# A second expert's weight load moved into the loop, the widest layer 1 block put first, registers read ahead, and fills placed anew

## The chip, the core and the metric

The kernel runs on one core of a Trainium2 chip. The metric is the device time of one execution in microseconds (us). Three timed runs of the kernel before gave 604.38, 605.06 and 607.2 us; the median is 605.06 us. A profiled execution, taken apart from these, took 608.49 us, and its span from the first to the last instruction is 606.7 us.

## The reference

Two stages are computed in float32. The first is a linear attention for 8 batches, 8 heads, 576 positions and a head size of 64; the second sends each of the 4608 resulting rows (512 wide) to the one expert of 8 that its gate prefers, and multiplies the expert's result by the gate's weight.

```python
q_s = softmax(q, axis=-1);  k_s = softmax(k, axis=2)
kv  = einsum('bhsd,bhse->bhde', k_s, v)
x   = einsum('bhsd,bhde->bhse', q_s, kv)      # 4608 rows of 512
expert_idx = argmax(x @ w_gate, axis=1);  gate_w = softmax(x @ w_gate)[expert_idx]
for e in range(8):                            # rows sorted by expert
    h = maximum(x_sorted[lo:hi] @ w1[e], 0)   # layer 1: 512 -> 1024
    y_sorted[lo:hi] = h @ w2[e]               # layer 2: 1024 -> 512
out = gate_w[:, None] * y                     # in the order of the rows
```

## The kernel before, in words

**First part (0 to 190 us of the span).** A planner (class `Plan`) knows every step of the attention, the routing and the first expert's start by a name, a batch and an index (`KM2.1.0` is step KM2 of batch 1). From costs and due times it writes one fixed order for each engine. Before a step on TensorE it can put fills: products of a matrix of ones, 384 columns wide, whose results nobody reads (line 227). The table `FILL` lists how many stand ahead of which step: `KM2.1.0.18` means 18. The finished rows are scattered to a table `xs` in device memory, sorted by expert. For the first expert the first 384 rows are loaded early, and layer 1 for them and a third of layer 2 belong to this part (lines 755 and 769).

**Second part (from 190 us on), function `experts`.** Each engine has its own program here, and semaphores tie them together. Before the loop TensorE does the other two thirds of the first expert's layer 2 (`first`, line 1131), and between them the 12 transposes of the loop's first tile of rows (line 1147). Then each engine walks a loop, one round for a tile of up to 384 rows. A table `tab` in SBUF, computed by the routing, holds for each round its width in units of 32 rows (`kind`, 1 to 12), its first row, and whether a new expert begins; engines read it into registers (line 1009).

In a round TensorE branches on `kind` to one of six blocks of code for layer 1: `tiny1` for up to 64 rows, or `layer1(w)` for a width of 256, 288, 320, 352 or 384. Every `layer1(w)` has 96 products (8 blocks of hidden units, 12 products each). After it come the three thirds of layer 2: 24 products (`layer2`) or 16 (`half`) for each 128 rows that the tile has. ScalarE applies the relu to each hidden block (line 1194), VectorE computes its low part (line 1281, semaphore `sHL[f]`). In the middle of the round VectorE transposes the next tile (line 1260), ScalarE rounds it (line 1178), and VectorE takes the low part (line 1266, semaphore `sXL`, on which the next round's layer 1 waits). ScalarE scales the results (line 1163), and GpSimd scatters them to the output (line 1368).

Weights are 2 MB for each layer of an expert, and come by SyncE's queue into `RAW1` and `RAW2` (lines 1420 and 1424), from which ScalarE and VectorE make the high and low parts W1H, W1L (lines 1231, 1334), W2H and W2L (lines 1187, 1272). The loop's first rounds belong to the first expert, whose weights have been there since the first part. SyncE loads the loop's first tile, then, before its loop, both weights of the second expert:

```python
with e.If(x.get(LIVE, 1, 0, 1) > 0):          # line 1445
    wload(x.get(EO, 1, 0, E - 1), False)
```

In each round it waits until the tile in use has been taken over (`sGS`), loads the next tile's rows (line 968), and, in the first round of a new expert, loads the weights of the one after, each when its buffer is free.

ScalarE begins a round with three reads of the table into registers (`kind`, `fresh`, `turn`) and does a fourth after the relus.

Of the kernel before, what the change touches and what calls it, by code (L numbers as in the profile page):

```python
# [16 lines left out]
P = 128  # L17
# [25 lines left out]
            T4=135.561, T5=67.264, T6=-338.231, T7=192.024, T8=-120.773, T9=1000.0, PD=179.626, SW=73.996)  # L43
WINDOW = 0.0
FILL = """
KM2.0.0.17 KM4.0.0.1 KM2.1.0.18 KM4.1.0.4 KV.0.0.1 KV.0.1.1 KM2.2.0.13 G2.0.0.1 KV.1.1.1 KV.1.2.1 KM2.3.0.4 G0.1.0.7
KM4.3.0.1 TR.1.2.1 KV.2.2.1 R5.0.0.2 MM.1.4.4 KV.3.2.1 G0.3.0.9 TR.3.2.1 G2.3.0.2 KV.4.0.1 KV.4.1.1 KV.4.2.1 KM2.5.0.16
KV.4.3.2 R5.2.0.1 MM.3.0.1 MM.3.1.2 MM.3.2.2 MM.3.3.2 TR.3.4.2 G2.4.0.2 KV.5.2.1 G2.5.0.2 MM.5.0.4 MM.5.1.4 TR.5.4.1
KM4.7.0.14 KV.6.0.1 KV.6.1.1 KV.6.2.1 G0.6.0.5 TR.6.2.2 IT.4.1.1 IT.4.2.4 MM.7.0.1 MM.7.4.2 KV.7.0.1 KV.7.1.1 KV.7.2.2
"""  # L50
KD, ROW, LW, EO, LIVE = range(5)
PE, DVE, ACTE, POOL, SP = "pe", "dve", "act", "pool", "sp"
# [919 lines left out]
def experts(nc, tc, g):  # L972


    NC, NF, DM, N, E = g.NC, g.NF, g.DM, g.N, g.E
# [3 lines left out]
    H2, Q = P // 2, P // 4  # L979
# [9 lines left out]
    sPH, sHH, sHL = [sem(x, NF) for x in ("sph", "shh", "shl")]  # L989
# [29 lines left out]
    def pe():  # L1019
        x = Eng(nc.tensor, "pe")  # L1020
        e = nc.tensor
# [37 lines left out]
        def tiny1():  # L1059
            for h in range(2):  # L1060
                e.wait_ge(sW1[2 * h], it)
                e.wait_ge(sW1[2 * h + 1], it)
                n = 0
                for c in range(NC):
                    for wt in (W1H, W1L):
                        m = e.matmul(g.PH[h], g.XH[:, c, :P], wt[:, c, h * DM:(h + 1) * DM], start=(n == 0), stop=(n == 2 * NC - 1))
                        if n == 0 and h == 0:
                            m.wait_op(sXL, it, GE)
                        n += 1
                m.then_inc(sPH[h], 1)  # L1070
            ones(4)
            for h in range(2):
                if h:
                    ones(3)
                for f in range(4 * h, 4 * h + 4):
                    m = e.matmul(TP[h][:, f - 4 * h, :], HS[:, f * P:(f + 1) * P], g.pair, start=True, stop=True)
                    if f == 4 * h:
                        m.wait_op(sHH[h], it, GE)
                m.then_inc(sPH[2 + h], 1)
            for f in range(4, NF):  # L1080
                e.sem_inc(sPH[f], 1)
# [18 lines left out]

        def body(j):
            kind = x.get(KD, j, 0, 12)
            with e.If(kind < 9):
                with e.If(kind < 3):
                    tiny1()
                with e.If(kind > 2):
                    layer1(2 * P)
            with e.If(kind > 8):
                with e.If(kind < 12):
                    with e.If(kind < 11):  # L1110
                        with e.If(kind < 10):
                            layer1(9 * Q)
                        with e.If(kind > 9):
                            layer1(10 * Q)
                    with e.If(kind > 10):
                        layer1(11 * Q)
                with e.If(kind > 11):
                    layer1(3 * P)
            for u in range(3):
                with e.If(kind > 4 * u + 2):  # L1120
                    layer2(u)
                with e.If(kind < 4 * u + 3):
                    with e.If(kind > 4 * u):
                        half(u)
            x.add("it", 1)
# [15 lines left out]
        it, hc = x.reg("it", 1), x.reg("hc", 1)  # L1141
# [10 lines left out]
    def act():  # L1152
        x = Eng(nc.scalar, "act")
        e = nc.scalar
        it, m1, m2 = x.reg("it", 1), x.reg("m1", 16), x.reg("m2", 16)
        cu = [x.reg(f"c{u}", 1) for u in range(3)]
        ou = [x.reg(f"o{u}", 16) for u in range(3)]

        def yout(u, again=True):
            if again:  # L1160
                e.wait_ge(sO[u], ou[u])
                x.add(f"o{u}", 16)
            m = e.activation(g.YT[u], g.PY[u], AF.Copy, scale=g.GA[:, u:u + 1]).wait_op(sPY[u], cu[u], GE)  # L1163
            m.then_inc(sYT[u], 1)
            x.add(f"c{u}", 1)

        def yhalf(u):
            e.wait_ge(sO[u], ou[u])
            x.add(f"o{u}", 16)
            for i, cols in enumerate(HALVES):  # L1170
                m = e.activation(g.YT[u][:H2, cols], g.PY[u][H2:, cols], AF.Copy, scale=g.GA[:H2, u:u + 1])
                if i == 0:
                    m.wait_op(sPY[u], cu[u], GE)
                m.then_inc(sYH, 1)
            x.add(f"c{u}", 1)

        def evac(to=g.XH, src=g.XR):
            e.activation(to, src, AF.Copy).wait_op(sT, it, GE).then_inc(sXH, 1)

        def gates():  # L1180
            e.wait_ge(sGS, it)
            for u in range(3):
                e.wait_ge(sYT[u], cu[u])
            e.activation(g.GA, g.GS[:, :, 0], AF.Copy).then_inc(sGA, 1)

        def w2_hi(f):
            m = e.activation(W2H[:, f, :], g.RAW2[:, f, :], AF.Copy)  # L1187
            if f == 0:
                m.wait_op(sR2, m2, GE)
            m.then_inc(sH2[f], 1)  # L1190

        def relus(split):
            for f in range(NF):
                e.activation(g.HH[:, f, :], g.PH[f][:, :W], AF.Relu).wait_op(sPH[f], it, GE).then_inc(sHH[f], 1)  # L1194
                if f == 0:
                    gates()
                if split:
                    w2_hi(f)

        def tiny(split):  # L1200
            w2 = (lambda *fs: [w2_hi(f) for f in fs]) if split else (lambda *fs: None)
            w2(0)
            e.activation(HS[:, :DM], g.PH[0], AF.Copy).wait_op(sPH[0], it, GE).then_inc(sHH[0], 1)
            w2(1)
            gates()
            w2(2)
            for h in range(2):
                e.activation(g.HH[:, 4 * h:4 * h + 4, :H2], TP[h], AF.Relu).wait_op(sPH[2 + h], it, GE).then_inc(sHH[2 + h], 1)
                w2(3 + h)
            w2(5, 6, 7)  # L1210
            for f in range(4, NF):
                e.sem_inc(sHH[f], 1)

        def body(j):
            kind = x.get(KD, j, 0, 12)
            fresh = x.get(LW, j, 0, 1)
            turn = x.get(LW, j + 1, 0, 1)
            for run in (tiny, relus):
                with e.If(kind > 2 if run is relus else kind < 3):
                    with e.If(fresh > 0):  # L1220
                        run(True)
                        x.add("m2", 16)
                    with e.If(fresh < 1):
                        run(False)
            x.add("it", 1)
            with e.If(x.get(KD, j + 1, 0, 12) > 0):
                evac()
            with e.If(turn > 0):
                for q in range(NQ):
                    sl = slice(2 * q * P, 2 * (q + 1) * P)  # L1230
                    m = e.activation(W1H[:, :, sl], g.RAW1[:, :, sl], AF.Copy)
                    if q == 0:
                        m.wait_op(sR1, m1, GE)
                    m.then_inc(sH1[q], 1)
                x.add("m1", 16)
            for u in range(3):
                with e.If(kind > 4 * u + 2):
                    yout(u)
                with e.If(kind < 4 * u + 3):
                    with e.If(kind > 4 * u):  # L1240
                        yhalf(u)

        for u in range(3):
            e.sem_inc(sYT[u], 1)
        yout(0, again=False)
        yout(1, again=False)
        evac(g.XH.rearrange("p c (u t) -> p u c t", t=P), g.PT)
        yout(2, again=False)
        x.walk(body)
        for u in range(3):  # L1250
            e.sem_inc(sSp2, 1).wait_op(sO[u], ou[u], GE)
# [141 lines left out]
    def sp():  # L1393
        x = Eng(nc.sync, "sp")
        e = nc.sync
# [33 lines left out]
        def body(j):  # L1429
            e.wait_ge(sGS, it)  # L1430
            rows(j + 1)
            with e.If(x.get(LW, j, 0, 1) > 0):
                x.add("k", 1)
                kk = e.snap(k, min_val=2, max_val=E)
                with e.If(x.get(LIVE, kk, 0, 1) > 0):
                    wload(x.get(EO, kk, 0, E - 1), True)
            x.add("it", 1)

        n, row = g.AT0
        for u in range(3):  # L1440
            with e.If(n > 4 * u):
                e.dma_start(g.XT[:, u, :], g.xs[bass.ds(row + u * P, P), :]).then_inc(sX, 16)
            with e.If(n < 4 * u + 1):
                e.sem_inc(sX, 16)
        with e.If(x.get(LIVE, 1, 0, 1) > 0):
            wload(x.get(EO, 1, 0, E - 1), False)
        x.walk(body)

    pe()
# [35 lines left out]
```

## Time and profile before

| what | value |
|---|---|
| timed runs | 604.38, 605.06, 607.2 us; median 605.06 us |
| profiled execution | 608.49 us; span 606.7 us |
| TensorE products busy | 575.0 us, 95% of the span |
| VectorE, ScalarE, GpSimd busy | 323.3, 237.0, 130.9 us |
| mean granted TensorE clock | 0.986 of full speed |
| data moved | 86.26 MB, 142 GB/s over the span |

TensorE is busy for nearly the whole span, so the time can shrink only where TensorE stands idle, runs at a lower clock, or does work that nobody needs. The profile cuts the span into 40 slices of 15.2 us; the clock's row is below full speed in a few slices between 150 and 230 us only. A busy share is a mean over a slice, and a stop of some microseconds is found in the chain of waits, the list that follows the last instruction back through what released each step.

### The profile page before, as it was taken

The page shows a single profiled execution, that of the slowest core. Times are in us where ns is not written, and L with a number is a line of the kernel's source. Part 1 is how long each engine was busy: PE and PEld are TensorE (multiplying, and loading weights), DVE is VectorE, ACT ScalarE, POOL GpSimd, SP SyncE. Part 2 cuts the span into 40 slices and gives each one's busy share as a digit, 9 for nine tenths or more (in the row PEclk, how much of TensorE's full clock was granted, in tenths as well). Part 3 has the DMA queues.
Part 4 walks back from the last instruction along what each step waited for, and adds up shares of the span by engine and source line. Part 5 has one row for each costly group of instructions (what it writes and reads, how often), then busy time and mean ns, then how long its engine had stood idle before and what let it go on. Part 6 is the DMA issues. An engine that isn't in the chain of part 4 may idle for free.

```text
span 606.7 us, 12049 instructions
## 1 busy us (share of the span) xinstructions
PE 575.0 (95%) x3858; PEld 501.4 (83%) x3859; DVE 323.3 (53%) x695; ACT 237.0 (39%) x492; POOL 130.9 (22%) x210
## 2 busy tenths in 40 slices
PE   7899999997999499999999999999999999999995
PEld 4677867776887398989989898989989898998983
DVE  6789989995890132252705041426552672566444
ACT  2566537663530112252412121325442542454344
POOL 3122556676250100101010101010101101010110
PEclk9999999999899889999999999999999999999998
DMA  9999998984553923016160302030634147053200
GB/s 262 294 268 242 307 303 227 274 252 173 193 202 118 334 36 70 36 29 213 59 184 0 87 17 70 17 87 6 208 133 104 52 156 226 9 193 143 67 17 22
DMA packets 85313, 86.26 MB, mean 142 GB/s; under 512 B 21024, under 2 KB 70688, under 8 KB 84641
## 3 DMA queue, kind: packets, MB, share of 16 engines
q1 hardware_dynamic: 79280, 66.82, 40.5%
q0 software_dynamic: 6000, 19.03, 8.6%
q8 instruction: 19, 0.31, 0.2%
q14 instruction: 14, 0.11, 0.1%
HBM read 63.88 MB, written 22.74 MB: 143 GB/s over the span
## 4 chain that ended last, share of the span: by engine, by line
PE 81%; DVE 7%; issue 4%; DMA 2%; ACT 2%; SPq 1%; POOL 1%; another core or an unknown queue 0%; DVEq 0%; POOLq 0%; ACTq 0%
PE py L1049 30%; PE pt L1033 23%; PE ph L1033 8%; PE xp L550 3%; PE kv L427 3%; DMA kt<-in_k 2%; PE ph L755 2%; PE py L1131 2%; PE qT L538 1%; PE py L1091 1%; PE kg L461 1%; PE xp L227 1%; DVE kp L375 1%; PE py L769 1%; DVE kt L409 1%
## 5 line engine op out<-in xcount | busy, mean ns | idle before, releaser
L1049 PE MATMUL py<-w2h,hid 128*128 128x512 f32 x528 | 164.8, 389 | 0.0
L1281 DVE SCALAR_TENSOR_TENSOR hid<-pt,hid 128x384 fp32r<-128x384 f32 x78 | 42.8, 557 | 186.9 <-ACT hid L1194 179.2
L1049 PEld LDWEIGHTS py<-w2h,hid 128*128 128x128 f32 x528 | 99.1, 188 | 20.1
L1368 POOL DMA_INDIRECT out<-yt,ix x39 | 42.5, 1089 | 316.4 <-ACT yt L1163 301.7
L1049 PE MATMUL py<-w2l,hid 128*128 128x512 f32 x264 | 102.7, 389 | 0.0
L1194 ACT ACTIVATE hid<-pt 128x384 fp32r<-128x384 f32 x78 | 38.3, 491 | 99.0 <-PE pt L1033 81.5
L1163 ACT ACTIVATE yt<-py,ga 128x512 f32<-128x512 f32 x36 | 24.7, 687 | 131.6 <-PE py L1049 117.9
L1033 PE MATMUL pt<-xh,w1h 128*128 128x384 f32 (+4 forms) x312 | 60.5, 316 | 8.2 <-issue 8.2
L1033 PE MATMUL pt<-xh,w1l 128*128 128x384 f32 (+4 forms) x312 | 59.9, 314 | 0.0
L1033 PE MATMUL pt<-xl,w1h 128*128 128x384 f32 (+4 forms) x312 | 59.9, 314 | 0.0
L1033 PEld LDWEIGHTS pt<-xh,w1h 128*128 128x128 f32 x312 | 51.2, 192 | 9.6 <-issue 8.6
L1049 PEld LDWEIGHTS py<-w2l,hid 128*128 128x128 f32 x264 | 49.6, 188 | 9.9
L1033 PEld LDWEIGHTS pt<-xl,w1h 128*128 128x128 f32 x312 | 50.3, 191 | 0.0
L1033 PEld LDWEIGHTS pt<-xh,w1l 128*128 128x128 f32 x312 | 50.3, 191 | 0.0
L663 POOL DMA_INDIRECT xs<-xr,posi x36 | 36.9, 1024 | 47.3 <-DVE lh L565 25.1
L1260 DVE STREAM_TRANSPOSE xrow<-xt 128x1536 f32<-128x1536 f32 x13 | 38.6, 2973 | 0.0
L550 PE MATMUL xp<-kx,qTs 128*128 128x146 f32 x256 | 37.3, 292 | 1.3 <-ACT kx L445 0.7
L550 PEld LDWEIGHTS xp<-kx,qTs 128*128 128x128 f32 x256 | 33.3, 190 | 3.9 <-issue 1.5
L543 ACT ACTIVATE qTs<-qT 128x512 f32<-128x512 f32 x36 | 21.1, 596 | 29.8 <-PE xp L550 15.8
L227 PEld LDWEIGHTS <-ones 128*128 128x128 bf16 x212 | 21.1, 102 | 14.1 <-issue 3.1
L497 POOL TENSOR_TENSOR qs<-qt,qm 128x1024 f32<-128x1024 f32 (+1 forms) x16 | 23.8, 1512 | 41.2 <-DVE qm L492 34.1
L1272 DVE TENSOR_TENSOR w2l<-raw,w2h 128x512 fp32r<-128x512 f32 x40 | 27.2, 689 | 6.9 <-ACT w2h L1187 6.7
(246 smaller groups left out, 883.3 us busy)
## 6 DMA issues: line engine op xcount, KB each, us to landing
raw<-in_moe_w SPq DMA_DIRECT2D x10, 2048.0 KB, 9.3
vt<-in_v SPq DMA_DIRECT2D x16, 512.0 KB
qt<-in_q SPq DMA_DIRECT2D x8, 1024.0 KB
kt<-in_k SPq DMA_DIRECT2D x7, 1024.0 KB
xt<-xs SPq DMA_DIRECT2D x32, 192.0 KB
xs<-zr SPq DMA_DIRECT2D x11, 260.0 KB
xt<-in_moe_w SPq DMA_DIRECT2D x8, 256.0 KB
raw<-in_moe_w SPq DMA_DIRECT2D x4, 512.0 KB
```

Source lines behind the costliest of these rows:

```text
L227: nc.tensor.matmul(hot.t if to is None else to, ones16, ones16[:, None, :].to_broadcast([P, HOT // P, P]), start=True, stop=True)
L497: nc.gpsimd.tensor_tensor(o.qs[:, j0:j1].rearrange("p j h d -> p h j d"), o.qt[:, :, j0:j1, :], o.qm[:, :, j0:j1, None].to_broadcast([P, H ...
L550: nc.tensor.matmul(xv[:, c, :KW], o.qT[i][:, c, :], kx[:, c, :], start=True, stop=True)
L663: s = nc.gpsimd.indirect_dma_start(out=xs, out_offset=bass.IndirectOffsetOnAxis(ap=n.pi[:, t - t0:t - t0 + 1], axis=0), in_=xr[:, t, :], i ...
L1033: m = e.matmul(ph, wt[:, c, f * P:(f + 1) * P], xt[:, c, :w], start=(n == 0), stop=(n == 3 * NC - 1))
L1049: m = e.matmul(g.PY[u], ht[:, f, u * P:(u + 1) * P], wt[:, f, :], start=(n == 0), stop=(n == 3 * NF - 1))
L1163: m = e.activation(g.YT[u], g.PY[u], AF.Copy, scale=g.GA[:, u:u + 1]).wait_op(sPY[u], cu[u], GE)
L1194: e.activation(g.HH[:, f, :], g.PH[f][:, :W], AF.Relu).wait_op(sPH[f], it, GE).then_inc(sHH[f], 1)
L1260: e.transpose(g.XR.rearrange("p c (k j) -> p k c j", j=32), xblocks(g.XT).rearrange("p k (l c) -> p k c l", c=NC)).wait_op(sX, ld, GE).the ...
L1272: m = e.tensor_tensor(W2L[:, f, :], g.RAW2[:, f, :], W2H[:, f, :].bitcast(F32), op=ALU.subtract).wait_op(sH2[f], n2, GE)
L1281: e.scalar_tensor_tensor(g.HL[:, f, :], g.PH[f][:, :W], 0.0, g.HH[:, f, :].bitcast(F32), op0=ALU.max, op1=ALU.subtract).wait_op(sHH[f], it ...
L1368: e.indirect_dma_start(out=g.out, out_offset=bass.IndirectOffsetOnAxis(ap=g.IX[:, u:u + 1], axis=0), in_=g.YT[u], in_offset=None, bounds_c ...
```

## The change

Four things are changed.

1. SyncE no longer loads the second expert's weights before its loop. In round 0 it loads the next tile first, then waits until VectorE has finished the last hidden block of that round (`sHL[7]`), and then issues both loads, 4 MB together, with no wait between them.
2. TensorE's branches on `kind` are turned round: the block for 384 rows stands first behind the loop's head, `tiny1` last.
3. ScalarE keeps `kind` and `fresh` of a round in two registers, which the round before has filled; it reads both entries of the next round after its relus, and copies them at the end of the round.
4. The table of fills is another: 196 fills in place of 172. The planned steps stand in the same order on every engine; the numbers of fills ahead of some differ. Ahead of steps of batches 0 to 2 stand 25 more (8 more at `KM2.1.0`, 6 at `KM4.1.0`, 5 at `KM2.2.0`, 3 at `KM4.0.0`); from batch 3 on there is one fewer in sum, with 4 new at `G0.7.0` and 4 fewer at `KM2.5.0`.

```diff
 FILL = """
-KM2.0.0.17 KM4.0.0.1 KM2.1.0.18 KM4.1.0.4 KV.0.0.1 KV.0.1.1 KM2.2.0.13 G2.0.0.1 KV.1.1.1 KV.1.2.1 KM2.3.0.4 G0.1.0.7
...
+KM2.0.0.17 KM4.0.0.4 KM2.1.0.26 KM4.1.0.10 KM2.2.0.18 KM4.2.0.1 KM2.3.0.2 G0.1.0.5 R5.0.0.2 MM.1.4.5 G0.3.0.9 G2.3.0.3
...
@@ TensorE, body of the loop
-            with e.If(kind < 9):
-                with e.If(kind < 3):
-                    tiny1()
-                with e.If(kind > 2):
-                    layer1(2 * P)
-            with e.If(kind > 8):
-                with e.If(kind < 12):
+            with e.If(kind > 11):
+                layer1(3 * P)
+            with e.If(kind < 12):
+                with e.If(kind > 8):
+                    with e.If(kind > 10):
+                        layer1(11 * Q)
                     with e.If(kind < 11):
+                        with e.If(kind > 9):
+                            layer1(10 * Q)
                         with e.If(kind < 10):
                             layer1(9 * Q)
-                        with e.If(kind > 9):
-                            layer1(10 * Q)
-                    with e.If(kind > 10):
-                        layer1(11 * Q)
-                with e.If(kind > 11):
-                    layer1(3 * P)
+                with e.If(kind < 9):
+                    with e.If(kind > 2):
+                        layer1(2 * P)
+                    with e.If(kind < 3):
+                        tiny1()
@@ ScalarE, body of the loop
-            kind = x.get(KD, j, 0, 12)
-            fresh = x.get(LW, j, 0, 1)
-            turn = x.get(LW, j + 1, 0, 1)
+            kind = e.snap(kd, min_val=0, max_val=12)
+            fresh = e.snap(lw, min_val=0, max_val=1)
...
-            with e.If(x.get(KD, j + 1, 0, 12) > 0):
+            more = x.get(KD, j + 1, 0, 12)
+            turn = x.get(LW, j + 1, 0, 1)
+            with e.If(more > 0):
                 evac()
...
+            e.reg_mov(kd, more)
+            e.reg_mov(lw, turn)
...
+        kd, lw = x.reg("kd", x.get(KD, 0, 0, 12)), x.reg("lw", x.get(LW, 0, 0, 1))
         x.walk(body)
@@ SyncE, body of the loop and what stands ahead of it
             rows(j + 1)
+            with e.If(j < 1):
+                with e.If(x.get(LIVE, 1, 0, 1) > 0):
+                    eo = x.get(EO, 1, 0, E - 1)
+                    e.wait_ge(sHL[NF - 1], it)
+                    wload(eo, False)
             with e.If(x.get(LW, j, 0, 1) > 0):
...
-        with e.If(x.get(LIVE, 1, 0, 1) > 0):
-            wload(x.get(EO, 1, 0, E - 1), False)
         x.walk(body)
```

TensorE, the head of the loop's body before: the read of `kind` (TENSOR_LOAD from the table), two branches, and the first block of code, which is `tiny1` (w1h and w1l are the parts of W1, xh the rows).

```order
L1016 UNCONDITIONAL_BRANCH
L1016 ISA
L1009 TENSOR_LOAD tab
L1009 ISA x2
L1103 COMPARE_AND_BRANCH
L1104 COMPARE_AND_BRANCH
L1066 MATMUL pt<-w1h_61,xh 128x512
L1066 MATMUL pt<-w1l_62,xh 128x512
```

TensorE, the same place now:

```order
L1017 UNCONDITIONAL_BRANCH
L1017 ISA
L1010 TENSOR_LOAD tab
L1010 ISA x2
L1104 COMPARE_AND_BRANCH
L1034 MATMUL pt<-xh,w1h_61 128x384 x4
L1034 MATMUL pt<-xl,w1h_61 128x384 x4
L1034 MATMUL pt<-xh,w1l_62 128x384 x4
```

The block for 384 rows moved from the end of the six to the place right behind the loop's head; before, it stood behind `tiny1` (31 products) and four blocks of 96.

SyncE, from the last row of the first tile's load to the head of its loop, before (raw1 and raw2 are the buffers of the raw weights):

```order
L1443 UNCONDITIONAL_BRANCH
L1009 TENSOR_LOAD tab_127
L1009 ISA x2
L1445 COMPARE_AND_BRANCH
L1009 TENSOR_LOAD tab_127
L1009 ISA x2
L1420 ISA
L1420 DMA raw1_2236<-in_moe_w1 128x4096
L1424 ISA
L1424 DMA raw2_2237<-in_moe_w2 128x8x512
L1445 UNCONDITIONAL_BRANCH
```

SyncE now, inside the body of the loop, behind the loads of the next tile's rows:

```order
L1437 COMPARE_AND_BRANCH
L1010 TENSOR_LOAD tab_127
L1010 ISA x2
L1438 COMPARE_AND_BRANCH
L1010 TENSOR_LOAD tab_127
L1010 ISA x2
L1425 ISA
L1425 DMA raw1_2261<-in_moe_w1 128x4096
L1429 ISA
L1429 DMA raw2_2262<-in_moe_w2 128x8x512
L1438 UNCONDITIONAL_BRANCH
```

The two loads passed the loop's entry and the first `rows(j + 1)` on SyncE's queue; the branch of line 1437 lets them happen in round 0 alone.

ScalarE, the head of its loop's body before, up to the first branches on `kind` and `fresh`:

```order
L1016 UNCONDITIONAL_BRANCH
L1016 ISA
L1009 TENSOR_LOAD tab
L1009 ISA x3
L1009 TENSOR_LOAD tab
L1009 ISA x3
L1009 TENSOR_LOAD tab
L1009 ISA x2
L1219 COMPARE_AND_BRANCH
L1220 COMPARE_AND_BRANCH
```

ScalarE, the same place now, from the reads ahead of the loop:

```order
L1010 TENSOR_LOAD tab
L1010 ISA x2
L1010 TENSOR_LOAD tab
L1010 ISA x2
L1013 TENSOR_LOAD tab
L1013 ISA x2
L1017 UNCONDITIONAL_BRANCH
L1017 ISA
L1219 COMPARE_AND_BRANCH
L1220 COMPARE_AND_BRANCH
```

The three reads of a round's head are gone from the body; two of them now stand once ahead of the loop, and in the body behind the relus.

## Rows read from the trace of the kernel before

**Rows 1.** The page: the granted clock's 40 slices, and the first instruction queue.

```profile
PEclk9999999999899889999999999999999999999998
...
q8 instruction: 19, 0.31, 0.2%
```

**Rows 2.** Chain of waits around the loop's entry: start us, length us, what.

```profile
190.27 0.84 issue
...
204.07 8.17 issue
212.24 8.71 PE pt L1033 x36
...
231.36 16.33 PE py L1049 x72
247.69 6.24 PE pt L1033 x36
```

**Rows 3.** Stretches: length, busy per engine, granted clock, DMA share, GB/s.

```profile
204.00:212.00 8.00, 0.07 (x1) 0.00 (x0) 0.00 (x0) 0.69 (x1) 0.98 (x1) 0.68 1.06 336
212.00:221.00 9.00, 8.76 (x38) 8.79 (x39) 1.12 (x2) 1.08 (x4) 0.19 (x1) 0.72 0.43 69
272.00:280.00 8.00, 8.00 (x37) 6.64 (x36) 0.98 (x1) 0.69 (x1) 2.81 (x2) 1.00 1.02 259
```

**Rows 4.** Timeline, VectorE, SyncE and GpSimd: start, length, instruction [idle before <-releaser].

```profile
196.74 0.39 SPq L1424 DMA_DIRECT2D raw<-in_moe_w  x1
...
202.17 1.76 DVE L1266 TENSOR_TENSOR xl<-pt,xh 128x1536 fp32r<-128x1536 f32 x1 [16.38 <-ACT xh L1178]
...
205.58 4.35 SPq L968 DMA_DIRECT2D xt<-xs  x4
...
214.56 0.19 POOL L1379 CAST ix<-gs 128x3 int32<-128x3 f32 x1 [7.91 <-DMA out<-yt,ix]
```

**Rows 5.** The page, DMA issues: count, KB, median us to landing.

```profile
raw<-in_moe_w SPq DMA_DIRECT2D x10, 2048.0 KB, 9.3
...
xt<-xs SPq DMA_DIRECT2D x32, 192.0 KB
...
out<-yt,ix POOLq DMA_INDIRECT x39, 2.7
```

**Rows 6.** Waits of TensorE from 215 us to the end: total, times, longest.

```profile
PE py L1091 <- issue: 0.3, 1, 0.3
```

**Rows 7.** Timeline of later rounds: SyncE, ScalarE and VectorE.

```profile
231.92 0.56 DVE L1281 SCALAR_TENSOR_TENSOR hid<-pt,hid 128x384 fp32r<-128x384 f32 x1 [1.52 <-ACT hid L1194]
237.04 2.38 SPq L968 DMA_DIRECT2D xt<-xs  x4
254.97 2.93 DVE L1260 STREAM_TRANSPOSE xrow<-xt 128x1536 f32<-128x1536 f32 x1
266.48 3.89 ACT L1231 ACTIVATE w1h<-raw 128x1024 fp32r<-128x1024 f32 x4
275.33 0.36 SPq L1420 DMA_DIRECT2D raw<-in_moe_w  x1
```

**Rows 8.** Timeline of TensorE, first part: fills, and idle times ahead of steps.

```profile
10.69 5.04 PE L227 MATMUL kmT<-ones 128*128 128x384 bf16 x30
17.00 0.63 PE L384 MATMUL kmT<-ident,km 128*128 128x128 f32 x4 [1.27 <-DVE km L379]
19.79 0.62 PE L393 MATMUL mb<-ident,mx 128*128 128x128 f32 x4 [0.70 <-DVE mx L388]
152.24 1.11 PE L452 MATMUL kvT<-ident,kx 128*128 128x128 f32 x4 [3.69 <-ACT qTs L543]
```

**Rows 9.** Timeline of the last round, from 588 us: ScalarE, TensorE, VectorE.

```profile
591.42 0.63 ACT L1187 ACTIVATE w2h<-raw 128x512 fp32r<-128x512 f32 x1 [2.24 <-issue]
591.72 0.39 PE L1066 MATMUL pt<-w1l,xh 128*128 128x512 f32 x1
592.69 0.68 DVE L1292 COPY xrow<-pt 128x512 f32<-128x512 f32 x1
```

More of the change, by code (lines that the diff above doesn't have):

```diff
@@ L45 @@
 FILL = """
-KM2.0.0.17 KM4.0.0.1 KM2.1.0.18 KM4.1.0.4 KV.0.0.1 KV.0.1.1 KM2.2.0.13 G2.0.0.1 KV.1.1.1 KV.1.2.1 KM2.3.0.4 G0.1.0.7
-KM4.3.0.1 TR.1.2.1 KV.2.2.1 R5.0.0.2 MM.1.4.4 KV.3.2.1 G0.3.0.9 TR.3.2.1 G2.3.0.2 KV.4.0.1 KV.4.1.1 KV.4.2.1 KM2.5.0.16
-KV.4.3.2 R5.2.0.1 MM.3.0.1 MM.3.1.2 MM.3.2.2 MM.3.3.2 TR.3.4.2 G2.4.0.2 KV.5.2.1 G2.5.0.2 MM.5.0.4 MM.5.1.4 TR.5.4.1
-KM4.7.0.14 KV.6.0.1 KV.6.1.1 KV.6.2.1 G0.6.0.5 TR.6.2.2 IT.4.1.1 IT.4.2.4 MM.7.0.1 MM.7.4.2 KV.7.0.1 KV.7.1.1 KV.7.2.2
+KM2.0.0.17 KM4.0.0.4 KM2.1.0.26 KM4.1.0.10 KM2.2.0.18 KM4.2.0.1 KM2.3.0.2 G0.1.0.5 R5.0.0.2 MM.1.4.5 G0.3.0.9 G2.3.0.3
+KM2.5.0.12 KV.4.3.1 MM.3.1.2 MM.3.3.3 TR.3.4.5 G2.4.0.2 G2.5.0.2 MM.5.0.4 MM.5.1.4 TR.5.4.1 KM4.7.0.14 G0.6.0.5
+TR.6.2.2 G2.6.0.2 KV.7.2.1 G0.7.0.4 IT.4.1.2 IT.4.2.2 MM.7.4.2 KV.0.1.1 KV.0.0.1 G2.0.0.1 KV.1.0.1 KV.1.1.3 G2.1.0.1
+KM4.3.0.1 TR.1.2.1 KV.2.2.1 KV.3.1.1 TR.3.2.1 KV.4.0.1 KV.4.1.2 R5.2.0.1 KV.5.2.1 KV.5.1.1 KV.6.0.1 KV.6.1.1 KV.6.2.1
+KV.7.1.1 G2.7.0.1
 """
```

## The prediction

> **What bounds the kernel now.** I read the page first. TensorE's products are busy for 575.0 of 606.7 us, 95% of the span (the table above), and the clock's 40 slices are full except from 152 to 167 us and from 197 to 227 us [rows 1]. So gains lie where TensorE stands idle or slow, and the chain of waits was next. At 204.07 us, where the loop is entered, it has a piece of 8.17 us called "issue", which means that TensorE waited for nothing that the profile shows; it is the longest such piece that falls on TensorE. The first 36 products of round 0 then take 8.71 us, the same 36 of round 1 only 6.24 [rows 2]. In round 1 and later nothing of this kind is left: from 215 us to the end TensorE's waits add up to 0.3 us [rows 6]. For a steady round TensorE is the bound, and what the other engines do faster there is worth nothing.
>
> The timeline says what the 8.17 us were not. VectorE's low part of the rows, on which layer 1 waits, ended at 202.17 + 1.76 = 203.93 us, before the last product of the part ahead [rows 4]. No data was late. The stretches say what went on beside it: SyncE had issued the second of the two weight loads, 4 MB together, at 196.74 us, and in 204 to 212 us the DMA engines were full (share 1.06, 336 GB/s) [rows 3, 4]. Everything small that used them was slow then: the scatter of results was waited for 7.91 us, until 214.56, against a median of 2.7 us to landing; and SyncE took 4.35 us for the four issues of the next tile, against 2.38 a round later [rows 4, 5, 7]. Code comes by DMA too: an instruction queue moved 0.31 MB in 19 packets, 16 KB each [rows 1]. So few packets in an execution of 14 rounds cannot be a new fetch of every engine's code in each round, so code is fetched about once. I read the piece as TensorE waiting for the code of its first layer 1 block, which lies behind `tiny1` and four blocks of 96 products, while 4 MB of weights were ahead of it.
>
> The Trainium skill, "Runtime: NRT & Kernel Launch", section "Instruction fetch mechanics", says that code is fetched by DMA in 16 KiB blocks, in sequence, and that a taken branch out of the resident window has to wait for its block. The packet size here agrees; that a far branch always costs a wait does not, since from 215 us on there are 0.3 us of waits in all [rows 6].
>
> **The change part by part.**
>
> *Loop entry.* Both edits at this place act on the same wait. The load is off the queues at 204 us, and the 384 block now stands right behind the loop's head, so that no branch is taken to it. Removed: 8.17 us of idle time. The clock in 204 to 212 us fell to a mean of 0.68, and was still 0.72 in 212 to 221 us, so half speed (the 1.2 GHz level) for part of it, after TensorE had done nothing [rows 3]; without the idle time the first 36 products should take what round 1 shows: 8.71 - 6.24 = 2.47 us more [rows 2]. What stays of the wait is not in the trace. Its lower bound is 0, as in every later round [rows 6]; the nearest row is the entry into this part of the program, 0.84 us at 190.27 with the DMA engines idle [rows 2]; the upper bound is the 8.17 itself. I take 0.5, between the two near ones. Sum: -8.17 - 2.47 + 0.5 = -10.1 us.
>
> *The moved load.* In round 0 it waits for VectorE's eighth low part, 231.92 + 0.56 = 232.48 us before, and so about 222.3 now. At the 9.3 us that a 2 MB load takes to landing, two in a row are there by 241 [rows 5]. The first use is ScalarE's rounding of W1 in round 1, at 266.48, now 256.3: 15 us of cover [rows 7]. SyncE's queue behind the waiting instruction holds only the next round's tile, issued at 237.04, now about 227, and used by VectorE's transpose at 254.97, now about 245 [rows 7]. Behind both loads it lands by 241 plus about 3.5 us (4 x 192 KB at the same rate), just in time; a microsecond late costs nothing, since layer 2 of that round has its own 16.3 us [rows 2]. The later loads stay where they are; one of them ran at a DMA share of 1.02 while TensorE was busy for the whole stretch [rows 3, 7]. Cost 0. If the cover were gone, each late microsecond would be one of idle TensorE.
>
> *The other five blocks and their order.* Every width now takes other branches, `tiny1` the longest. By the same 0.3 us the branches of all widths, first visits among them, are hidden behind products already issued [rows 6]. Cost 0; bounds -0.3 and, for the last round's `tiny1`, +0.84 from the nearest row [rows 2].
>
> *ScalarE's registers.* In a steady round this is hidden. In the last round it is not: ScalarE ends its scaling at 591.42 - 2.24 = 589.18 and begins the next operation at 591.42, an idle 2.24 us with no releaser [rows 9]. Three reads of the table stand there, and go. What follows (W2's low parts on VectorE) waits for it, but VectorE also needs TensorE's second half of layer 1, which ends at 591.72 + 0.39 = 592.11, and copies it from 592.69 [rows 9]. So at most 592.69 - 592.11, 0.6 us, of the 2.24 reach the end. I take -0.6; bounds 0 and -0.6.
>
> *Fills.* One costs 5.04 / 30 = 0.168 us [rows 8]. 24 more are 4.0 us if each delays the chain, which is the upper bound. 25 more stand in batches 0 to 2, where TensorE waits for others: the 8 at `KM2.1.0` (1.34 us) meet 1.27 us of idle time, the 6 at `KM4.1.0` (1.0) meet 0.70 [rows 8]. That leaves about 0.4 us, and as much again for places without a row of their own. After that there is one fill fewer in sum; the 4 new ones at `G0.7.0` fall into an idle 3.69 us at 148.5 to 152.24 [rows 8], after which the clock was low. They could keep some of it up, so the bound below zero is 1.5 us. The clock stood at its full digit before that [rows 1], so early fills have nothing to win. I take +0.5: most of the added fills stand where idle time covers them.
>
> *The sum.* -10.1 - 0.6 + 0.5 = -10.2 us, made against the profiled execution's 608.49 us, which gives 598.3. The timed median is 605.06, 3.4 us lower. Taken over whole, 594.9. But waits on a full DMA queue are what differs most from one execution to the next, and part of those 3.4 us may have been in this one; I give back 0.6 of them and forecast 595.5 us.
>
> **The rivals.**
>
> *The same stop at another place.* Round 0 now has its far branch behind layer 1, over the five other blocks to layer 2, and that is just where the 4 MB begin. For it: the load alone was enough to make a wait of microseconds [rows 3, 4]. Against it: layer 1 ends at 231.36 and the wait is released 1.1 us later [rows 2, 7], before the load has even been issued, and a single load's full share left TensorE busy [rows 3]. Price: the stop returns whole, 8.17 + 2.47, so 605.06 + 0.5 - 0.6 = 605 us.
>
> *The wait is not the load's.* If entering the loop costs 8 us by itself (reading the count, the first reads of the table), it stays. For it: "issue" names no releaser, and the entry happens once. Against it: the 0.84 us for the entry at 190.27, and the scatter and SyncE, slow at the same time. Price: the 10.1 us stay, 605 us.
>
> *Slower.* The 4 MB, never issued back to back inside a round before, catch two first fetches of code in round 0's layer 2: the branch to it, and one over the skipped `half` code. Each costs 8.17 + 2.47 = 10.64, one is saved: 605.06 + 10.64 - 0.1 = 615.6 us. It decides if the branch's fetch is still under way when the load's packets begin, some 1.1 us after layer 1; against it speaks that the loads in later rounds met such short branches without a wait [rows 6].
>
> *Fills at full price.* 605.06 - 10.1 - 0.6 + 4.0 = 598.4, still faster.
>
> The skill's rule on taken branches, in the section named above, would add a wait for `tiny1` in the last round, since its block is now the farthest one. By the trace's nearest row that would be the 0.84 us already taken as a bound, which makes 596.3 us; I give it one in six, within the forecast.
>
> **How the numbers follow.** Forecast (with either price of the fills) 0.81, the same stop elsewhere 0.08, not the load's 0.06, slower 0.05. What this kernel's measurement can tell from no change is 0.5%, 3 us: below 602.0 is faster, above 608.1 slower. The forecast's cases end between 591 and 602 (residual wait 0 to 3 us, fills -1.5 to +4). Of its 0.81 I leave 0.01 for a residual wait beyond that, which ends within the 3 us; so faster 0.80, same 0.15 (0.08 + 0.06 + 0.01), slower 0.05. The range reaches from 591 to 602.5; the two cases at 605 and the slower one are left outside.
>
> **What would show it.** Right: no piece of "issue" over 1 us in the chain at the loop's entry; the first 36 products of round 0 in about 6.3 us at full clock; both weight issues about 10 us before 232, and TensorE without idle time in layer 2 of round 0. The DMA share high from about 224 to 240 us. ScalarE's gap in the last round below 1 us. Wrong: a new piece of idle TensorE between layer 1 and layer 2 of round 0, or W1's rounding in round 1 waiting for its load; an entry still 5 us long; the first part ending more than 2 us later than at 190 us.

## The result and the profile after

The changed kernel took 595.85 us (median of 4 runs, 595.35 to 596.0) against 606.12 us for the kernel before in the same comparison (4 runs, 604.38 to 607.2). The ratio is 0.9832 with a 95% interval of 0.9802 to 0.9861: 10.3 us faster. The forecast was 595.5 us, 9.6 us less than the median of 605.06 us that was known then. The span of the profiled executions went from 606.7 to 594.0 us.

The chain of waits of the changed kernel around the loop's entry and in two later places (start us, length us, what) answers to [rows 2]:

```profile
186.09 0.84 issue
...
196.46 3.43 PE py L1132 x15
199.89 6.42 PE pt L1034 x36
...
216.72 0.51 issue
217.23 16.61 PE py L1050 x72
...
379.81 1.00 issue
380.81 11.16 PE py L1050 x48
```

The piece of 8.17 us is gone: layer 1 of round 0 follows the last product of the part ahead without a gap, and its first 36 products take 6.42 us in place of 8.71. Two small pieces are new, 0.51 us between layer 1 and layer 2 of round 0 and 1.00 us at the same place of a later round. TensorE's waits of the second part, as totals, answer to [rows 6]; the second row is in the last round:

```profile
PE py L1050 <- issue: 1.5, 2, 1.0
PE py L1092 <- DVE w2l L1277: 0.5, 1, 0.5
```

The page's clock row has no slice below its full digit now, against four in [rows 1] (one of them the span's last slice, which the account of before leaves out):

```profile
PEclk9999999999999999999999999999999999999999
```

The stretches (columns as in [rows 3]) and the timeline show where the 4 MB went:

```profile
216.00:224.00 8.00, 7.49 (x35) 6.03 (x34) 2.38 (x3) 2.67 (x3) 0.00 (x0) 1.00 0.65 229
224.00:232.00 8.00, 8.00 (x37) 6.64 (x36) 0.00 (x0) 0.69 (x1) 1.96 (x2) 1.00 1.01 352
```

```profile
218.02 0.36 SPq L1425 DMA_DIRECT2D raw<-in_moe_w  x1
...
223.03 7.33 SPq L969 DMA_DIRECT2D xt<-xs  x4
...
241.12 2.94 DVE L1265 STREAM_TRANSPOSE xrow<-xt 128x1536 f32<-128x1536 f32 x1
...
253.27 3.88 ACT L1233 ACTIVATE w1h<-raw 128x1024 fp32r<-128x1024 f32 x4
```

The load fills the DMA engines from 224 to 232 us while TensorE is busy for all of it. SyncE's next four issues now take 7.33 us (in [rows 7] 2.38), but VectorE's transpose of that tile and ScalarE's rounding of W1 have no idle time before them: the cover was long enough.

The profile gives more than the times do. From the first product of line 769 (770 in the changed kernel) to the end of the span there are 606.7 - 184.55 = 422.15 us before and 594.0 - 180.37 = 413.63 now, 8.5 us less. The other 4.2 us of the 12.7 came in the first part; whether they belong to the change is the question of the fills.

### The profile page after: what moved, and what is told of

Read it like the earlier page. It is cut to its first block, busy times and chain, and to the rows that moved or that the text cites. A ratio compares the mean times of both kernels' runs of the same rounds, so it can differ in the third digit from the quotient of the medians.

```text
span 594.0 us, 12021 instructions
## 1 busy us (share of the span) xinstructions
PE 574.8 (97%) x3882; PEld 499.9 (84%) x3883; DVE 324.7 (55%) x695; ACT 237.2 (40%) x492; POOL 131.5 (22%) x210
## 3 DMA queue, kind: packets, MB, share of 16 engines
q0 software_dynamic: 6000, 19.03, 8.7%
## 4 chain that ended last, share of the span: by engine, by line
PE 86%; DVE 9%; issue 2%; ACT 1%; DMA 1%; POOL 0%; DVEq 0%; SPq 0%; POOLq 0%; ACTq 0%
PE py L1050 30%; PE pt L1034 24%; PE ph L1034 8%; PE kv L428 4%; PE xp L551 3%; PE ph L756 2%; PE py L1132 2%; PE qT L539 2%; DVE qm L493 2%; PE kmT L228 1%; PE py L1092 1%; PE py L770 1%; DVE xr L568 1%; DVE km L377 1%; PE qT L228 1%
## 5 line engine op out<-in xcount | busy, mean ns | idle before, releaser
L228 PEld LDWEIGHTS <-ones 128*128 128x128 bf16 x236 | 23.2, 101 | 15.3 <-issue 2.9
L1271 DVE TENSOR_TENSOR xl<-xrow,xh 128x1536 fp32r<-128x1536 f32 x12 | 21.1, 1759 | 18.6 <-ACT xh L1179 18.6
```

The lines of the kernel that those rows point to most:

```text
L228: nc.tensor.matmul(hot.t if to is None else to, ones16, ones16[:, None, :].to_broadcast([P, HOT // P, P]), start=True, stop=True)
```

## The experiments

The runs of one comparison share a chip and its runs of the kernel before. Three comparisons were made, in which the kernel before had medians of 611.8, 613.0 and 604.8 us; so ratios are compared, not times. The length of the second part (from the first product of line 769 to the end of the span) is taken from each profile, since the first part's length differs between executions by more than most edits do.

**Fills alone.** The table of fills is the new one, nothing else.

> Only the table of fills is the new one. In the changed kernel's profile the first part ended 4.2 us earlier than before (186.09 against 190.27), and the stop of all engines between 143 and 152 us was gone. Theory A: the fills did that, since they move every later piece of TensorE's code; then this kernel is 3 to 4 us faster than before, its first part ends near 186 us, and the 8.2 us at the loop's entry stay. Theory B, that of the prediction: fills cost about 0.5 us and the stop comes and goes from one execution to the next; then the time is within 1 us of before.

Ratio 0.991 (0.9882 to 0.9938), 606.97 against 611.79 us. Its chain at the loop's entry:

```profile
208.71 5.33 issue
214.05 8.33 PE pt L1034 x36
```

The time is 4.8 us less (3.8 to 7.2 by the interval), more than either theory had. The first part did not get shorter (189.19 us to line 770, against 188.62 in the run with the registers alone), and the stop of all engines was there, so theory A's account falls; theory B's 1 us falls with the time. What is shorter is the entry's piece, 5.33 us instead of about 8, and with it the second part, by 3.2 us. The fills change the amount of code ahead of the branch and no instruction behind it. That this is what shortened the piece was not shown; it may also be the spread between executions.

**The load alone.** SyncE's two hunks of the diff, the old order of blocks, the old registers and fills.

> Only the second expert's load is moved into round 0; the 384 block stays the farthest. Theory: the wait at the loop's entry was a fetch of code behind 4 MB of weights; then the far branch alone costs at most 1 us, the piece at the entry falls from 8.2 to 1 us or less, the clock stays up, and the kernel is 9 to 10 us faster. Rival: a far first branch costs 8 us by itself; then the piece stays and the time is that of before.

Ratio 0.992 (0.9889 to 0.995), 606.53 us.

```profile
209.08 2.71 issue
211.79 6.50 PE pt L1033 x36
```

Without the load, with the DMA engines at a share of 0.16 in 204 to 212 us, the far branch still costs 2.71 us. So the load made about two thirds of the wait, not all but 1 us of it: the theory's mechanism holds, its number does not, and the rival's "8 us by itself" falls. The time is 5.3 us less (3.1 to 6.8 by the interval) where 9 to 10 were expected; the profile's second part is 7.7 us shorter than before.

**The order of blocks alone.** TensorE's hunk, with the load left ahead of the loop.

> Only the order of the six layer 1 blocks is changed; the 4 MB still load across the loop's entry. Theory: no branch out of the sequence is taken there, so the entry's piece is under 1.5 us although the DMA engines are full; the far branch comes 17 us later, behind layer 1, when the load has landed; 8 to 10 us faster. Rival: fetches in sequence wait behind the load as well; then 4 to 8 us stay at the entry or inside layer 1 of round 0.

Ratio 0.9899 (0.9858 to 0.9941), 605.77 us.

```profile
207.25 3.43 PE py L1131 x15
210.68 6.42 PE pt L1033 x36
...
227.50 0.79 issue
```

```profile
204.00:212.00 8.00, 8.00 (x43) 6.82 (x43) 1.82 (x2) 2.63 (x3) 0.99 (x1) 1.00 0.88 328
212.00:220.00 8.00, 8.00 (x48) 8.00 (x47) 1.67 (x3) 2.06 (x5) 1.17 (x2) 1.00 1.10 312
```

TensorE enters the loop and runs layer 1 without a gap although the DMA engines were full for 16 us. The first instruction queue, which brings TensorE's code (see below), has one packet in this time, at 208.4 to 209.4 us, and none after it until 225.2. So the rival, that fetches in sequence wait as well, was put to the test by one packet only; the other code was there already. The time is 6.0 us less (3.6 to 8.7) where 8 to 10 were expected.

Either edit alone removes most of the wait. By the second parts of the profiles the load alone gives 7.7 us, the order alone 8.1, and both with the registers 8.5 (the run with all but the fills, below): not additive. The times alone don't show it; they give 5.3, 6.0 and 9.2 us, with intervals 4 to 6 us wide.

**ScalarE's registers alone.**

> Only ScalarE's registers are read ahead. Theory from the changed kernel's last round: ScalarE's idle 2.24 us falls to 0.5, but the products that TensorE has queued ahead of the transposes set the end, so 0.1 us is won and the time is that of before within 0.5 us. The prediction had 0.6 us. It also repeats the first part of before: if the stop at 143 to 152 us belongs to the old fills' code it is there again.

Ratio 1.0002 (0.9974 to 1.0031). The entry's piece is 7.67 us, and the last round, from its first product to the start of its last scatter, takes 606.00 - 591.82 = 14.18 us. In the kernel before it took 602.56 - 588.29 = 14.27:

```profile
588.29 0.39 PE L1066 MATMUL pt<-w1h,xh 128*128 128x512 f32 x1
...
602.56 0.99 POOL out L1368
```

The stop at 148 to 154 us was there too.

**Half the load ahead of the loop** (W1 there, W2 in round 0):

```diff
-            wload(x.get(EO, 1, 0, E - 1), False)
+            e.dma_start(g.RAW1, w1v[...]).then_inc(sR1, 16)      # ahead of the loop
+                    e.wait_ge(sHL[NF - 1], it)                   # in round 0
+                    e.dma_start(g.RAW2, w2v[...]).then_inc(sR2, 16)
```

> The kernel before, but only the load of W1 (2 MB) stands ahead of the loop; that of W2 moves into round 0. Theory: the fetch for the far branch waits behind what is queued, so the piece at the entry lies between 2.7 us (no load) and 8.2 us (4 MB), near 4 to 5 us, and the clock falls for a while. If any load at all blocks it as 4 MB do: 7 to 8 us. If 2 MB are no hindrance: 2.7 us.

Ratio 0.9976 (0.9952 to 1.0), 602.83 against 604.79 us.

```profile
200.47 5.01 issue
205.49 8.46 PE pt L1033 x36
```

The piece lies between those with no load and with the whole one, as expected. But it is close to the 5.33 us of the run with the fills alone, which had the whole load, so these runs don't part 2 MB from 4 MB.

**The kernel before, profiled again:**

> The kernel before, profiled again on the chip of these runs. If the entry's piece is a property of the kernel it is 7 to 9 us again, and from the first product of line 769 to the end are about 422 us; the first part ends 4 us later than in the first profile, as in the other runs of this chip, whatever its fills.

It took 604.14 us in its one run.

```profile
179.66 5.72 PE py L769 x24
...
199.19 9.45 issue
208.64 7.94 PE pt L1033 x36
```

The wait at the entry is the kernel's: 8.17, 7.67 and 9.45 us in three profiles with the old order, the old fills and the whole load (the second of them the run with the registers alone), and 5.33 in a fourth, with the new fills. With 0, 2 and 4 MB ahead of it the far branch waits 2.71, 5.01 and 5.3 to 9.5 us. The second part is 602.3 - 179.66 = 422.64 us, as expected. The last forecast of this run failed, and tells most: with the old fills the first part ended at 179.66, before the changed kernel's 180.37.

**What the wait waits for.** The DMA records of the traces hold the packets of code themselves. The first queue of kind "instruction", q8 ([rows 1]), moves packets of 16 KB, and its packets go with TensorE's stops, from which it is read here as TensorE's. In the kernel before it moves nothing from 203 to 207.6 us, and two packets from 207.6 to 210.4 us, in the middle of the stop:

```profile
q8 instruction: 2, 0.03, 8.3%
```

Every profile with the old order has such a pair at the entry (us from the span's start; the run of the last row is described below):

| run | load ahead | TensorE's last product ends | pair of code packets | next product |
|---|---|---|---|---|
| before | 4 MB | 204.07 | 207.70 to 210.36 | 212.24 |
| before, again | 4 MB | 199.19 | 204.13 to 206.93 | 208.64 |
| registers alone | 4 MB | 208.16 | 211.36 to 214.17 | 215.83 |
| fills alone | 4 MB | 208.71 | 209.40 to 212.32 | 214.05 |
| half the load | 2 MB | 200.47 | 200.91 to 203.57 | 205.49 |
| load alone moved | none | 209.08 | 207.49 to 210.07 | 211.79 |
| early load, old order | none | 210.05 | 208.34 to 211.11 | 212.76 |

The pair takes 2.6 to 2.9 us everywhere, and the next product starts 1.6 to 1.9 us after it. What differs is when it starts: 1.6 and 1.7 us before TensorE's last product ends where no load stands ahead, and 0.4 to 4.9 us after it where one does. So the load made the wait by holding back the start of the code's packets. Why they came early in the run with the fills is open.

**The load made to meet the far branch.** In the changed kernel it waits for the third hidden block instead of the eighth:

```diff
-                    e.wait_ge(sHL[NF - 1], it)
+                    e.wait_ge(sHL[2], it)
```

> The changed kernel, but the load waits for the third hidden block's low part instead of the eighth, so that the 4 MB are under way when TensorE takes its first branch from the 384 block over five others to layer 2. If a first far branch under load is what cost 8 us before, the stop comes back at that place: 4 to 8 us idle between layer 1 and layer 2 of round 0, a slow clock after it, 4 to 10 us slower than the changed kernel. This is the slower rival's mechanism made to happen. If the load does not matter there: the 0.5 us that the changed kernel shows.

606.42 us against 602.8 for the changed kernel in the same comparison. The chain, and the stretches after it:

```profile
215.52 6.24 PE pt L1034 x36
221.76 3.73 issue
225.49 19.03 PE py L1050 x72
```

```profile
220.00:224.00 4.00, 1.76 (x11) 1.44 (x9) 1.12 (x2) 1.54 (x3) 0.00 (x0) 0.98 1.04 393
224.00:228.00 4.00, 2.51 (x6) 2.06 (x7) 1.83 (x2) 0.64 (x1) 0.00 (x0) 0.50 0.26 96
```

The stop comes back behind layer 1: 3.73 us, a little under the 4 expected, and then the clock at half speed, with layer 2 at 19.03 us in place of 16.6. The time, 3.6 us more than the changed kernel's, is a little under the expected range too. The packet of code before layer 2 comes at 222.59 to 223.55 us, after layer 1 has ended at 221.76; in the changed kernel's first profile it comes at 214.43 to 215.30, before layer 1 ends at 216.72. From its end to layer 2 are 1.9 us both times.

**The same early load with the old order of blocks:**

> The same early load, but the old order of blocks, where the 384 block stands last and layer 2 follows it without a branch. If branch and load must meet: no wait between layer 1 and layer 2 although the DMA engines are full there, and 2 to 3 us at the loop's entry, where the far branch meets no load (2.7 us in the run with the load moved alone). If the load alone stops TensorE: idle time in round 0 as in the other run.

```profile
210.05 2.71 issue
212.76 8.04 PE pt L1034 x36
...
224.96 6.24 PE pt L1034 x36
231.20 16.33 PE py L1050 x72
```

```profile
228.00:232.00 4.00, 4.00 (x24) 3.84 (x23) 0.95 (x3) 0.98 (x2) 0.00 (x0) 1.00 0.97 380
```

With the DMA engines at 0.97 TensorE goes from layer 1 to layer 2 without a gap, since here no far branch stands between them; the far branch at the entry, which meets no load, costs the same 2.71 us as in the run with the load alone. The time is 607.14 us. Branch and load must meet for the long stop: each of the four combinations has now been seen at each of two places.

**The changed kernel again, and all of it but the fills:**

> The changed kernel again, on the chip of these runs, with a second profile. From the first pair: no piece at the loop's entry, 0.5 us at the first branch from layer 1 to layer 2, 8.5 us less from the end of the first part to the end. What the first part gives is open: if the new fills earn 4 us there by themselves, the whole is 12 us faster; if that was one execution's luck, 8 to 9 us.

> The changed kernel with the old table of fills. The loop's entry is clean in both, so the difference to the changed kernel is what the fills are worth. Theory A (the fills gave the first part's 4.2 us): 3 to 4 us slower than the changed kernel, the stop of all engines near 150 us back. Theory B (fills cost or give little, as predicted): within 1 us of it.

Ratios to the kernel before 0.981 (0.9767 to 0.9854) and 0.984 (0.9788 to 0.9892), 602.8 and 603.82 us, against 613.04 us: the medians put the fills at 1 us, and the intervals overlap. The whole is 10.2 us faster by the medians, between the two cases that were expected. The second profile of the changed kernel has 1.06 us at the first branch and 603.2 - 188.45 = 414.75 us in the second part, 7.4 us less than the first profile of before. The first parts reach line 770 at 188.45 and line 769 at 188.55 us. And the stop of all engines that the changed kernel's first profile lacked stands in its second profile, while the kernel before, profiled again, is without it. The rows 148 to 154 us are the changed kernel's second profile and the second of the kernel before, in this order (in [rows 8] the stop shows as 3.69 us ahead of 152.24):

```profile
148.00:154.00 6.00, 5.08 (x38) 4.20 (x37) 3.37 (x12) 3.23 (x11) 5.13 (x10) 1.00 0.46 178
154.00:160.00 6.00, 4.18 (x17) 3.33 (x18) 2.14 (x7) 1.91 (x4) 0.15 (x2) 0.62 0.13 47
```

```profile
148.00:154.00 6.00, 5.78 (x50) 4.55 (x50) 5.15 (x17) 3.98 (x9) 2.10 (x5) 1.00 0.56 209
```

The stop does not follow the fills. In the eight profiles of the first two comparisons, with either table, TensorE is idle for 1.9 us or more between 142 and 160 us; in the three of the last comparison, two with the old fills and one with the new, for 0.2 to 0.3 us. There the first parts end at 179.66 and 180.95 us with the old fills and at 179.86 with the new. So the 4.2 us of the first pair of profiles were not the fills'. What stops all engines there was not looked into.

**Without the products of ones in the last round:**

```diff
                 m.then_inc(sPH[h], 1)
-            ones(4)
             for h in range(2):
```

> The changed kernel without the four products of ones between the last round's layer 1 and its transposes. Theory: these stood between ScalarE's earlier copy and the end, so the transposes start 0.65 us sooner and the last round, from its first product to its last scatter, takes 13.5 us instead of 14.2; the time falls by 0.5 us, which 5 rounds hardly show. Rival: VectorE's eight low parts of W2 set the end; then the last round stays at 14.2 us.

594.97 us, ratio to the kernel before 0.9844 (0.983 to 0.9858). It did not share a chip with the changed kernel, so that the times don't rank the two; the last round is measured in the profiles. The changed kernel, ScalarE, TensorE and the last scatter:

```profile
575.70 0.39 PE L1067 MATMUL pt<-w1h,xh 128*128 128x512 f32 x1
...
577.12 0.63 ACT L1188 ACTIVATE w2h<-raw 128x512 fp32r<-128x512 f32 x1 [0.53 <-issue]
...
579.35 0.82 PE L1058 MATMUL ph<-ones 128*128 128x384 bf16 x4
579.55 0.69 DVE L1297 COPY xrow<-pt 128x512 f32<-128x512 f32 x1 [1.07 <-PE pt L1067]
580.01 1.00 PE L1077 MATMUL pt<-pair,xrow 128*128 128x64 f32 x8
...
589.87 0.98 POOL L1373 DMA_INDIRECT out<-yt,ix  x1 [7.34 <-DVE yt L1350]
```

and without the four products:

```profile
575.43 0.39 PE L1067 MATMUL pt<-w1h,xh 128*128 128x512 f32 x1
...
579.08 1.00 PE L1076 MATMUL pt<-pair,xrow 128*128 128x64 f32 x8
...
588.94 0.98 POOL L1372 DMA_INDIRECT out<-yt,ix  x1 [7.21 <-DVE yt L1349]
```

From the first product to the last scatter 14.17 us become 13.51: the four products were what the end waited for.

## Why the prediction was right, and where its terms were not

*Where the time was.* The 8.17 us at the entry, the slow clock behind it, and the reading of both as a branch to code that was fetched behind 4 MB of weights: shown, by taking the load away, by taking the branch away, by making the two meet at another place, and by the packets of code, which start late in every stop with a load. Halving the load adds little, as its 5.01 us are close to the 5.33 that the whole load gave once. The term of 10.6 us (8.17 + 2.47) came out as 8.17 + (8.71 - 6.42) = 10.5.

*What is left of the wait.* Here a step failed in size: +0.5 us were put in, and branches of all widths were costed at nothing "by the same 0.3 us". They were hidden before, but the 384 block now ends in a far branch to layer 2 that is taken for the first time in round 0. The changed kernel shows 0.51 us there with 16.61 - 16.33 = 0.28 us behind it, and 1.00 + (11.16 - 10.91) at the first such branch of the 320 block (10.91 is that layer 2 in the kernel before): 2.0 us in all, 2.6 us of waits alone in its second profile. The row of 0.3 us was taken from 215 us on in the old order, where the last packet of code comes at 241 to 242 us: later branches there found their code, and the row says nothing on a branch that has to fetch. The changed kernel fetches four more, from 366 to 392 us, in the round that first runs the 320 block. The rivals' stop "at another place" is thus real, with 0.79 us of its 10.64, and the run with the early load shows what it would have been.

*The load alone* would not have done it to within 1 us: 2.71 us stay. The prediction did not need to part the two edits, because both were made.

*ScalarE's registers* were put at -0.6 us and gave -0.1 (14.27 to 14.18 and 14.17 us). The idle 2.24 us fell to 0.53, as said, and VectorE's copy came 0.55 us earlier; but next in line were four products of ones ahead of the transposes, which the prediction did not look at. Taking those away gave the 0.66 us.

*The fills* were put at +0.5. With the entry clean they come out at about -1 us, with intervals too wide to tell it from nothing or from +0.5; with the old entry they gave 4.8 us, of which the profile shows 3.2 at the entry, and why is open. That none of the 4.2 us of the first profile belong to them rests on the first parts of the later profiles.

*The sum.* The second part was forecast 10.7 us shorter without the fills and is 7.4 to 9.0 shorter between the two profiles of each kernel, 8.5 in the first pair. The times say 10.3 us, with an interval from 8.4 to 12.0 on the 606.12 us. The median was hit so closely because two misses, 1.5 us of first branches and 0.5 us of the last round, were about made up by the 0.6 us held back for the difference between profile and times, by the fills, and by what the first part happened to take in the runs compared. The comparison's median for the kernel before, 606.12 us, also lies 1.1 us above the one that the forecast started from. The mechanism was read rightly; the agreement to 0.4 us was luck.

*The slower rival* did not come: the wait was released at 218.0 us, after TensorE had begun layer 2 at 217.23, so the far branch was past. With the load issued 7.8 us after the start of layer 1 in place of 18.1, it was not past, and the kernel gave back 3.6 us of its 10.

## What to carry to other kernels

A piece of TensorE's time that waits for nothing in the profile, right at a first jump to far code, is worth reading together with the DMA share of that stretch: small transfers that are slow at the same time are a sign, and packets of the instruction queue that come late, inside the stop, confirm it. Either put the block that is taken first behind the jump, or keep big loads off the queues until the first pass through the code is over; one is enough for most of it. When a wait goes, look at what stands next in line on the same engine before the gain is counted, and do not take a first part's length from one profile.

## What was not expected of the hardware

The two packets of code for the entry's branch took 2.6 to 2.9 us whether the DMA engines were full or nearly idle; a load ahead of them delayed their start. With no load ahead the branch still cost 2.71 us, twice the same value, and a branch over as many blocks behind layer 1, whose last packet had come 1.4 us before layer 1's end, cost 0.51 us.

Later rounds take as far branches at no visible cost; the Trainium skill, "Runtime: NRT & Kernel Launch", section "Instruction fetch mechanics", has the wait, and the trace agrees where packets of code come, and shows no wait at such branches where none come. Having run before is not enough: the first branch from the 320 block to layer 2 waited 1.00 us, with a packet of code at 378.1 to 379.1 us, though five rounds had run that layer 2.

After the wait of 2.71 us the granted clock was 1.00 over the first 36 products in one run, which took 6.50 us, and 0.79 in the other, where they took 8.04. It stayed at full speed, the 2.4 GHz level, after the 0.83 to 0.87 us at the entry into the second part in every profile, and was at half speed, 1.2 GHz, after each of the stops of 3.73 us and more at the loop.
